# Splitting the first token block's hidden columns into two stretches around the second block, in a retention-plus-two-feed-forward kernel

## The chip, the cores and the metric

The kernel runs on one core of one Trainium2 chip. The metric is the device time of one execution in microseconds. Before the change the median of three runs is 911.7 us (911.51 to 911.89).

## What is computed

Three layers in float32, one after the other. Retention over 4 sequences of 768 tokens with 8 heads of width 64: per head `state = gamma*state + k v^T`, `y = scale * q state`. Then `x = elu(x @ w_in) @ w_out` with 512 to 2048 to 512 on all 3072 tokens. Then 512 to 1024 to 512 with `h * softmax(h)`, a layer norm over the 1024, a gain `g_ln`, and `@ w_out2`.

## The kernel before

**Arithmetic.** TensorE multiplies in fp32r. To keep float32 accuracy every operand is cut into a high part (a rounded copy) and a low part (the difference), and each product is three matmuls (`mm3`, lines 69 to 71). Weights arrive as raw 64-bit words, two uint32 each, and are made into float32 by bit operations. One weight tile (128x512) takes: a load on SP's queue (`load_w`, L97), absolute value on ScalarE (L102), a clamp on GpSimd (L103), three bit operations on VectorE (`bits_w`, L108 to L110), a high copy on ScalarE (`high_w`, L119) and a low difference on VectorE (`low_w`, L127). For the first feed-forward layer there are 32 such tiles: 16 of `w1i`, 16 of `w1o`.

**Retention.** The tokens of a sequence are cut into chunks of 64; a chunk of all heads is a *unit*, 48 in all, eight to a block of 512 tokens. For unit u: `scale_k` (GpSimd, L169), `att_scores` (TensorE, L175, L179), `att_mask` (VectorE, L183), `att_values` (TensorE, L216, L219), `att_done` (VectorE, L224, writes the unit's 64 columns of x), and `att_state` (VectorE L196, two small ScalarE copies L199, GpSimd L203). The state of unit u+1 needs that of unit u.

**First feed-forward layer.** Six blocks of 512 tokens, each 16 *steps*, one for each 128 hidden columns. Step s: `ff1_in` is 12 matmuls of 128x512 into a PSUM bank `hp`; `elu_a` to `elu_c` make the activation and its halves `gh` and `gl`; `ff1_out` of step s-2 (LAG = 2) adds 12 matmuls into `acc` (four banks that collect over the 16 steps of a block). After a block's last step the four banks are copied out by ScalarE and VectorE (L304, L306) and go to DRAM (`y_dr`).

**Order.** Everything stands in a `manual_schedule`: each engine issues its instructions in the order in which the program emits them, so an instruction that waits holds up all behind it on its engine; SP's DMA queue too. Tiles take any free buffer of their pool.

- Start: the eight units of block 0 in a loop (L442), with parts of three weights' conversion between them (`PRE`, `prep_w`) and the split of x in three pieces (`split_x0`, L244, L245), two of them on GpSimd. Units' inputs have four buffers and are loaded three units ahead.
- Block 0 (16 steps): two `prep_w` slots in every step convert two weights in a staggered manner: within a slot, the high copy of weight n-2, then the bit operations of n, then the low part of n-2. Every second step holds one unit of block 1. The activation goes by ScalarE twice (L262, L263), VectorE once (L272); `gl` by VectorE (L284).
- Blocks 1 to 5: the weights stay in SBUF. Every second step has one unit of the next block; `gl` by GpSimd. At the last step of a block the whole x of the next block is split: four ScalarE copies (L232), four VectorE differences (L237).
- Block 5 also converts the 16 weights of the second layer, one `prep_w` slot a step (those of `w_out2` are multiplied by the gain, L116), and reads back the first y tiles.
- Then the second feed-forward layer, 24 tiles of 128 tokens (`ff2_in`, `norm_a`, `norm_b`, `turn`, `turned`, `ff2_out`).

Of the kernel before, what the change touches and what calls it, by code (L numbers as in the profile page):

```python
# [18 lines left out]
P = 128  # L19
# [5 lines left out]
C = 64  # L25
# [10 lines left out]
HL = NF1 - 2  # L36
PRE = (2, 3, 4, 5)
AHEAD = 1
# [4 lines left out]
def tile_retention_ffn(ctx, tc, qkv, w_in1, w_out1, w_in2, w_out2, g_ln, dmask, odec, kdec, gdec, ident_in, out):  # L43
# [13 lines left out]
    xf = const.tile([P, KD, TB], F32, name="xf")  # L57
# [5 lines left out]

    t_dr = [dram.tile([4, 4, 32, 2 * P], F32, name=f"t_dr{i}") for i in range(3)]
# [8 lines left out]
    with tc.manual_schedule():  # L73
# [7 lines left out]
        x_p = ph1.enter_context(tc.tile_pool(name="x", bufs=1))  # L81
        e_p = ph1.enter_context(tc.tile_pool(name="e", bufs=3))
        g_p = ph1.enter_context(tc.tile_pool(name="g", bufs=3))
# [3 lines left out]
        stage_p = ph0.enter_context(tc.tile_pool(name="stage", bufs=4, side="right"))  # L87
# [18 lines left out]
        def bits_w(x):  # L106
            t, b = raw_t.pop(x), abs_t[x]
            nc.vector.tensor_scalar(b, b, 3, 0x3FFFFFF8, ALU.logical_shift_left, ALU.bitwise_and)  # L108
            nc.vector.scalar_tensor_tensor(b, t[:, :, 1], 0xC0000000, b, ALU.bitwise_and, ALU.bitwise_or)  # L109
            nc.vector.scalar_tensor_tensor(b, t[:, :, 0], 29, b, ALU.logical_shift_right, ALU.bitwise_or)  # L110
# [19 lines left out]
        def prep_w(order, n):  # L130

            at = lambda i: order[i] if 0 <= i < len(order) else None
            if at(n - 2):
                high_w(at(n - 2))
            if at(n + 1):
                clamp_w(at(n + 1))
            if at(n):
                bits_w(at(n))
            if at(n - 2):
                low_w(at(n - 2))  # L140
            if at(n + 3):
                load_w(at(n + 3))
# [19 lines left out]
        def load_unit(u):  # L162
            t = at_p.tile([P, 18 * D], F32, tag="in", name="in", bufs=4)
            nc.sync.dma_start(out=t, in_=qkv[u])
            in_t[u] = t
# [55 lines left out]
        def att_done(u, v):  # L221
            ci = u % UPB
            four = lambda t: t.rearrange("p (a o) t -> p a o t", a=2)
            nc.vector.tensor_tensor(four(xf[:, :, ci * C:(ci + 1) * C]), v[:, :, 2 * C:4 * C].rearrange("p a (o t) -> p a o t", o=2), four(od_sb), ALU.mult)  # L224

        x_t = {}

        def split_xh(tb, cs):
            if tb not in x_t:
                x_t[tb] = [x_p.tile([P, KD, TB], F32R, tag=tag, name=tag) for tag in ("xh", "xl")]  # L230
            for cc in cs:
                nc.scalar.copy(x_t[tb][0][:, cc], xf[:, cc])  # L232

        def split_xl(tb, cs):
            xh, xl = x_t[tb]
            for cc in cs:
                nc.vector.tensor_tensor(xl[:, cc], xf[:, cc], xh.bitcast(F32)[:, cc], ALU.subtract)  # L237


        def split_x0(ts, engine):  # L240
            if 0 not in x_t:
                x_t[0] = [x_p.tile([P, KD, TB], F32R, tag=tag, name=tag) for tag in ("xh", "xl")]
            xh, xl = x_t[0]
            nc.scalar.copy(xh[:, :, ts], xf[:, :, ts])  # L244
            engine.tensor_tensor(xl[:, :, ts], xf[:, :, ts], xh.bitcast(F32)[:, :, ts], ALU.subtract)  # L245
# [3 lines left out]
        def ff1_in(s):  # L249
            tb, f = divmod(s, NF1)  # L250
# [17 lines left out]
        def elu_b(s, on_act):  # L268
# [9 lines left out]
            if not on_act:  # L278
                elu_c(s, nc.gpsimd)
# [7 lines left out]
        def new_acc(tb):  # L287
            acc_t[tb] = [ps.tile([P, 2, 512], F32, tag="acc", name="acc", bufs=2) for _ in range(KD // 2)]

        def ff1_out(s):  # L290
            tb, f = divmod(s, NF1)
            if tb not in acc_t:
                new_acc(tb)
            wh, wl = w1o[f]
            gh, gl = g_t.pop(s)
            for m in range(KD):
                o = m * P
                mm3(acc_t[tb][m // 2][:, m % 2], wh[:, o:o + P], wl[:, o:o + P], gh, gl, f == 0, f == NF1 - 1)
            if f == NF1 - 1:
                for m in range(KD):  # L300
                    yt = yt_p.tile([P, TB], F32, tag="yt", name="yt", bufs=3) if m < 3 else e_p.tile([P, TB], F32, tag="e", name="yt")
                    src = acc_t[tb][m // 2][:, m % 2]
                    if m % 2:
# [3 lines left out]
                    nc.sync.dma_start(out=y_dr[tb][:, :, m, :].rearrange("c p t -> p c t"), in_=yt.rearrange("p (c t) -> p c t", c=CPB))  # L307
                del acc_t[tb]
# [30 lines left out]
        def norm_a(i):  # L339
            hp = h2.pop(i)  # L340
            st = sm_p.tile([P, 8], F32, tag="st", name="st")
            if i == 0:
                e, z = xf[:, :2], xf[:, 2:]
# [25 lines left out]
        def turn(i):  # L369
# [3 lines left out]
            t = z_p.tile([P, NF2 * P], F32, tag="t", name="t") if i else xf[:, :2].rearrange("p a b -> p (a b)")  # L373
# [51 lines left out]
        nc.gpsimd.memset(half_n, -0.5)  # L425
        load_unit(0)
# [7 lines left out]
        both = sets[0]  # L434
        scale_k(0)
# [4 lines left out]
        load_unit(2)  # L440
        slot = -1
        for u in range(UPB):  # L442
            nxt = sets[(u + 1) % 3] if u + 1 < UPB else both
            scale_k(u + 2)
            if u + 1 < UPB:
                att_scores(u + 1, nxt[0])
                att_mask(u + 1, nxt[1])
            if u + 3 < UPB + 3:
                load_unit(u + 3)
            if u < 2:  # L450
                load_w(order1[u])
# [4 lines left out]
            att_done(u, sets[u % 3][1])  # L456
            att_state(u + 1, nxt[1])
            if u in (3, 5, 7):
                split_x0(slice(0 if u == 3 else C * (u - 1), C * (u + 1)), nc.vector if u == 7 else nc.gpsimd)
            if u in PRE:  # L460
                prep_w(order1, slot)
                slot += 1


        NS = NB * NF1
        for s in range(NS + LAG):
            tb, k = divmod(s, NF1)
            u = UPB + AHEAD + s // 2 if s % 2 else (UPB if s == 0 else NU)
            if s < NS:
                ff1_in(s)  # L470
                elu_a(s, tb == 0)
                if k == NF1 - 1 and tb + 1 < NB:
                    split_xh(tb + 1, range(KD))
                    elu_b(s, tb == 0)
                    split_xl(tb + 1, range(KD))
            if u < NU:
                if u + 1 < NU:
                    att_scores(u + 1, both[0])
                att_values(u, both[0])
                if u + 1 < NU:  # L480
                    att_mask(u + 1, both[1])
                att_done(u, both[1])
                if u + 1 < NU:
                    att_state(u + 1, both[1])
                if u + 3 < NU:
                    load_unit(u + 3)
                if u + 2 < NU:
                    scale_k(u + 2)
            if tb == 0:
                prep_w(order1, slot)  # L490
                slot += 1
            if s < NS and (k < NF1 - 1 or tb + 1 == NB):
                elu_b(s, tb == 0)
            if s == NS + LAG - 2:
                ff2_in(0)
                norm_a(0)
                turn(0)
                turned(0)
                norm_b(0)
# [3 lines left out]
            if tb == 0:  # L503
# [131 lines left out]
```

## Time and profile before

| | |
|---|---|
| median of three runs | 911.7 us |
| the profiled execution's own time | 912.42 us |
| its span in the trace | 910.6 us |
| TensorE busy | 95% of the span, granted clock 0.979 in the mean |
| VectorE, ScalarE, GpSimd busy | 52%, 35%, 35% |

The 1.8 us between the span and the execution's time lie around the traced instructions. Shares of busy time are means over stages: block 0's steps lie between 37 and 159 us of the span, blocks 1 to 5 between 159 and 640, the second layer behind.

### The profile page before, as it was taken

What the parts mean: (1) busy time and instruction counts of PE and PEld (TensorE: products, weight loads), DVE (VectorE), ACT (ScalarE), POOL (GpSimd) and SP (SyncE); (2) the same over time, 40 slices, a digit from 0 to 9 for tenths busy, and PEclk for the clock granted to TensorE, in tenths of its full rate; (3) what the DMA queues carried; (4) which work ended last, traced back from release to release, by engine and by line L of the source; (5) the groups of instructions that cost most, each with busy time, mean ns of one, the idle gap of its engine ahead of it and who ended that gap; (6) DMA issues with size and microseconds to landing.
All of it is one profiled execution on the core that took longest, in us unless ns stands there. A gap on an engine that the chain in (4) does not pass through costs nothing.

```text
span 910.6 us, 15639 instructions
## 1 busy us (share of the span) xinstructions
PE 869.3 (95%) x6432; PEld 705.0 (77%) x6432; DVE 471.9 (52%) x781; ACT 320.2 (35%) x574; POOL 319.4 (35%) x319
## 2 busy tenths in 40 slices
PE   5588988999999999999999999999999999999998
PEld 4466766888888888888888887888778888888886
DVE  3589999422242223222432227899655555555442
ACT  3255555322232223222322223443333333333332
POOL 4434342333233323232333223455243333444330
PEclk9589999999999999999999999999999999999999
DMA  8445643211122111311131014330354444444432
GB/s 327 166 158 178 199 158 123 74 52 54 53 71 82 53 46 35 99 53 54 53 99 53 11 61 130 113 93 24 115 166 149 150 148 140 139 139 142 156 118 70
DMA packets 59879, 97.94 MB, mean 108 GB/s; under 512 B 4896, under 2 KB 41504, under 8 KB 59808
## 3 DMA queue, kind: packets, MB, share of 16 engines
q1 hardware_dynamic: 59808, 96.95, 32.5%
q8 instruction: 50, 0.82, 0.4%
q14 instruction: 21, 0.17, 0.1%
HBM read 72.29 MB, written 24.64 MB: 106 GB/s over the span
## 4 chain that ended last, share of the span: by engine, by line
PE 78%; DVE 14%; DMA 3%; issue 2%; ACT 1%; POOL 0%; SPq 0%; ACTq 0%; DVEq 0%; POOLq 0%
PE hp L70 12%; PE hp L71 12%; PE hp L69 12%; PE acc L69 9%; PE acc L70 8%; PE acc L71 8%; PE op L71 4%; PE op L69 4%; PE op L70 4%; DVE wt L109 3%; DVE wt L110 2%; PE ab L175 1%; DVE wt L108 1%; DMA in<-in_qkv 1%; DVE w1il L127 1%
## 5 line engine op out<-in xcount | busy, mean ns | idle before, releaser
L284 POOL TENSOR_TENSOR gl<-e,gh 128x512 fp32r<-128x512 f32 x80 | 107.5, 1344 | 225.0 <-issue 151.3
L71 PE MATMUL acc<-gh,w1ol 128*128 128x512 f32 x384 | 152.0, 396 | 8.1 <-DVE w1ol L127 8.1
L69 PE MATMUL hp<-xh,w1ih 128*128 128x512 f32 x384 | 152.2, 396 | 5.8 <-ACT xh L244 2.5
L69 PE MATMUL acc<-gh,w1oh 128*128 128x512 f32 x384 | 155.0, 404 | 2.0 <-ACT w1oh L119 2.0
L71 PE MATMUL hp<-xh,w1il 128*128 128x512 f32 x384 | 152.2, 396 | 1.0 <-DVE w1il L127 1.0
L70 PE MATMUL hp<-xl,w1ih 128*128 128x512 f32 x384 | 151.8, 395 | 0.9 <-DVE xl L237 0.9
L70 PE MATMUL acc<-gl,w1oh 128*128 128x512 f32 x384 | 151.0, 393 | 0.0
L265 ACT ACTIVATE e<-hp 128x512 f32<-128x512 f32 x80 | 47.8, 598 | 199.5 <-PE hp L71 197.7
L274 DVE TENSOR_SCALAR e<-e 128x512 f32<-128x512 f32 x80 | 35.5, 443 | 137.0 <-ACT e L265 137.0
L276 ACT CAST gh<-e 128x512 fp32r<-128x512 f32 x96 | 59.6, 621 | 118.9 <-DVE e L275 81.7
L71 PEld LDWEIGHTS acc<-gh,w1ol 128*128 128x128 f32 x384 | 72.8, 190 | 26.5 <-DVE w1ol L127 11.1
L183 DVE TENSOR_TENSOR pt<-ab,dm_sb 128x256 f32<-128x256 f32 x43 | 18.1, 422 | 142.5 <-PE ab L219 133.5
L69 PEld LDWEIGHTS hp<-xh,w1ih 128*128 128x128 f32 x384 | 73.4, 191 | 21.7 <-ACT xh L244 2.7
L71 PEld LDWEIGHTS hp<-xh,w1il 128*128 128x128 f32 x384 | 73.2, 191 | 19.2 <-DVE w1il L127 4.0
L69 PEld LDWEIGHTS acc<-gh,w1oh 128*128 128x128 f32 x384 | 72.5, 189 | 19.5 <-ACT w1oh L119 3.2
L70 PEld LDWEIGHTS hp<-xl,w1ih 128*128 128x128 f32 x384 | 73.3, 191 | 17.4 <-DVE xl L237 1.6
L70 PEld LDWEIGHTS acc<-gl,w1oh 128*128 128x128 f32 x384 | 72.7, 189 | 14.1
L354 POOL TENSOR_SCALAR z<-z,st 128x1024 f32<-128x1024 f32 x22 | 27.7, 1259 | 140.0 <-DVE st L352 140.0
L71 PE MATMUL op<-w2oh,zl 128*128 128x512 f32 (+1 forms) x192 | 74.2, 386 | 2.6 <-DVE zl L395 2.6
L69 PE MATMUL op<-w2oh,zh 128*128 128x512 f32 (+1 forms) x192 | 74.3, 387 | 0.6 <-ACT zh L389 0.6
L69 PE MATMUL hp<-w2ih,yh 128*128 128x512 f32 x192 | 74.7, 389 | 0.0
L70 PE MATMUL hp<-w2il,yh 128*128 128x512 f32 x192 | 74.7, 389 | 0.0
(112 smaller groups left out, 1408.2 us busy)
## 6 DMA issues: line engine op xcount, KB each, us to landing
in<-in_qkv SPq DMA_DIRECT2D x48, 576.0 KB, 4.2
raw<-in_w_in SPq DMA_DIRECT2D x24, 512.0 KB, 3.7
raw<-in_w_out SPq DMA_DIRECT2D x24, 512.0 KB, 3.5
t_dr<-t SPq DMA_DIRECT2D x22, 512.0 KB, 2.8
zt<-t_dr SPq DMA_DIRECT2D x88, 128.0 KB, 2.5
y_dr<-yt SPq DMA_DIRECT2D x24, 256.0 KB, 2.6
yin<-y_dr SPq DMA_DIRECT2D x24, 256.0 KB, 3.5
out<-ot SPq DMA_DIRECT2D x23, 256.0 KB, 2.7
```

What stands on the lines that cost most here:

```text
L69: nc.tensor.matmul(o, lh, rh, start=first, stop=False)
L70: nc.tensor.matmul(o, lh, rl, start=False, stop=False)
L71: nc.tensor.matmul(o, ll, rh, start=False, stop=last)
L108: nc.vector.tensor_scalar(b, b, 3, 0x3FFFFFF8, ALU.logical_shift_left, ALU.bitwise_and)
L109: nc.vector.scalar_tensor_tensor(b, t[:, :, 1], 0xC0000000, b, ALU.bitwise_and, ALU.bitwise_or)
L110: nc.vector.scalar_tensor_tensor(b, t[:, :, 0], 29, b, ALU.logical_shift_right, ALU.bitwise_or)
L183: nc.vector.tensor_tensor(pt, v[:, :, :2 * C], dm_sb, ALU.mult)
L265: nc.scalar.activation(e, h_t[s], AF.Exp)
L274: nc.vector.tensor_scalar(e, e, 1.0, -1.0, ALU.min, ALU.add)
L276: nc.scalar.copy(gh, e)
L284: engine.tensor_tensor(gl, e, gh.bitcast(F32), ALU.subtract)
L354: nc.gpsimd.tensor_scalar(z, z, st[:, 5:6], 1.0, ALU.add, ALU.mult)
```

## The change

The 96 steps of the first layer are ordered in segments: block 0's hidden columns 0 to 4, then the whole of block 1 (16 steps), then block 0's columns 5 to 15, then blocks 2 to 5. The sums of the first segment go to DRAM (`p_dr`, four tiles), are read back, and are added by VectorE when the third segment's banks are copied out. x is split unit by unit straight from `att_done`, and its two halves have two buffers each; the tile `xf` is gone. A generator deals a weight's work out in four parts (clamp of the next and first bit operation; second; third, the load of the weight three on, and the high copy; the low part), a number of parts at two places of a step: four and four in the first five steps, then four and two in even steps and two and two in odd ones through step 20. Before the first step one weight is converted instead of parts of three. All of block 0's units are loaded up front, in four buffers of a pool of their own and three others. Units of block 1 are worked in the first five steps (one in steps 0 and 1, two in steps 2 to 4), those of block 2 one a step in steps 21 to 28, the rest every second step.

```diff
-HL = NF1 - 2
-PRE = (2, 3, 4, 5)
-AHEAD = 1
+LEAD = 5
+SEGS = [(0, 0, LEAD), (1, 0, NF1), (0, LEAD, NF1)] + [(tb, 0, NF1) for tb in range(2, NB)]
+STEPS = [(i, tb, f) for i, (tb, a, b) in enumerate(SEGS) for f in range(a, b)]
...
-        x_p = ph1.enter_context(tc.tile_pool(name="x", bufs=1))
+        x_p = ph1.enter_context(tc.tile_pool(name="x", bufs=2))
...
-        stage_p = ph0.enter_context(tc.tile_pool(name="stage", bufs=4, side="right"))
+        stage_p = ph0.enter_context(tc.tile_pool(name="stage", bufs=3, side="right"))
...
+        def convert(order, held):
+            for n, x in enumerate(order):
+                if n:
+                    low_w(order[n - 1])
+                    yield
+                if n + 1 < len(order) and n + 1 != held:
+                    clamp_w(order[n + 1])
+                for i in range(3):
+                    bits_w(x, i)
+                    if i < 2:
+                        yield
+                if n + 3 < len(order):
+                    load_w(order[n + 3])
+                high_w(x)
+                yield
+            low_w(order[-1])
+
+        def run(turns, k):
+            for _ in range(k):
+                next(turns, None)
...
-        def att_done(u, v):
+        def att_done(u, v, engine):
...
+            xu = at_p.tile([P, KD, C], F32, tag="xu", name="xu")
+            nc.vector.tensor_tensor(four(xu), v[:, :, 2 * C:4 * C].rearrange("p a (o t) -> p a o t", o=2), four(od_sb), ALU.mult)
+            nc.scalar.copy(xh[:, :, ts], xu)
+            return lambda: engine.tensor_tensor(xl[:, :, ts], xu, xh.bitcast(F32)[:, :, ts], ALU.subtract)
...
+                    if i == 2:
+                        nc.vector.tensor_tensor(yt, src, back[m], ALU.add)
...
+                    if i == 0:
+                        nc.sync.dma_start(out=p_dr[m], in_=yt)
...
+        load_w(order1[0])
+        for u in range(2, UPB):
+            load_unit(u)
+        load_w(order1[1])
+        load_w(order1[2])
...
+            if u in (3, 4, 5, 6):
+                run(turns, 1)
...
+        slots = [(s, x) for s in range(LEAD) for x in (range(2) if s >= 2 * LEAD - UPB else range(1))]
+        slots += [(LEAD + NF1 + i, 0) for i in range(UPB)]
+        slots += [(s, 0) for s in range(2 * NF1, (NB - 1) * NF1, 2)]
...
+            if s <= END1:
+                run(turns, 4 if s < LEAD or s % 2 == 0 else 2)
...
+            if (s, 0) in bursts:
+                burst(bursts[s, 0])
...
+            if s <= END1:
+                run(turns, 4 if s < LEAD else 2)
+            if seg == 0:
                 elu_c(s, nc.vector)
+            if (s, 1) in bursts:
+                burst(bursts[s, 1])
```

## Rows read from the trace of the kernel before

**Rows 1.** The page: busy time of each engine, and the chain that ended last

```profile
PE 869.3 (95%) x6432; PEld 705.0 (77%) x6432; DVE 471.9 (52%) x781; ACT 320.2 (35%) x574; POOL 319.4 (35%) x319
PE 78%; DVE 14%; DMA 3%; issue 2%; ACT 1%; POOL 0%; SPq 0%; ACTq 0%; DVEq 0%; POOLq 0%
```

**Rows 2.** Windows: stretch, length, busy us (instructions) by engine, TensorE's granted clock, DMA

```profile
0.00:10.00 10.00, 3.62 (x94) 2.88 (x96) 1.73 (x5) 1.88 (x3) 2.56 (x9) 1.00 0.80 271
10.00:20.00 10.00, 7.59 (x253) 6.32 (x248) 5.43 (x13) 4.09 (x11) 5.71 (x9) 0.83 1.01 390
20.00:37.20 17.20, 6.31 (x193) 5.39 (x193) 11.75 (x21) 5.93 (x14) 12.94 (x13) 0.59 0.69 244
37.20:54.70 17.50, 13.94 (x152) 9.72 (x152) 9.12 (x14) 5.67 (x11) 4.86 (x5) 0.62 0.31 118
54.70:158.60 103.90, 93.12 (x765) 70.21 (x757) 100.62 (x159) 59.47 (x112) 35.66 (x37) 0.97 0.49 163
158.60:256.50 97.90, 97.46 (x864) 79.26 (x865) 32.15 (x67) 28.51 (x56) 29.38 (x30) 1.00 0.19 60
```

**Rows 3.** Waits of TensorE from 0 to 158.6 us: total, times, longest

```profile
PE acc L71 <- DVE w1ol L127: 8.1, 7, 1.5
PE ab L175 <- DMA in<-in_qkv: 5.1, 2, 4.7
```

**Rows 4.** Timeline of VectorE: states of the second and third unit

```profile
9.80 0.41 DVE L196 TENSOR_TENSOR state<-sg,acc 128x256 f32<-128x256 f32 x1
12.28 0.41 DVE L196 TENSOR_TENSOR state<-sg,acc 128x256 f32<-128x256 f32 x1
```

**Rows 5.** The chain that ended last, two steps of block 0

```profile
97.96 0.41 DVE pt L183
99.03 0.35 DVE wt L108
...
103.15 0.35 DVE wt L108
...
105.54 0.54 DVE gl L284
...
113.17 0.41 DVE pt L183
```

**Rows 6.** Groups of VectorE, 54 to 158 us: count, busy us, mean ns

```profile
L284 DVE TENSOR_TENSOR gl<-e,gh 128x512 fp32r<-128x512 f32 x14 | 15.0, 1070 | 0.0
L272 DVE SCALAR_TENSOR_TENSOR e<-e,hp 128x512 f32<-128x512 f32 x14 | 9.5, 675 | 0.0
```

**Rows 7.** Timeline of VectorE: a low part right behind its high copy

```profile
648.56 1.53 DVE L127 TENSOR_TENSOR w2ol<-wt,w2oh 128x512 fp32r<-128x512 f32 x1 [0.69 <-ACT w2oh L119]
```

**Rows 8.** Groups of VectorE, then of GpSimd, 596 to 638 us (block 5)

```profile
L110 DVE SCALAR_TENSOR_TENSOR wt<-raw,wt 128x512 uint32<-128x512 uint32 x8 | 12.6, 1580 | 0.3
...
L127 DVE TENSOR_TENSOR w2ol<-wt,w2oh 128x512 fp32r<-128x512 f32 x6 | 5.7, 956 | 0.0
L284 POOL TENSOR_TENSOR gl<-e,gh 128x512 fp32r<-128x512 f32 x8 | 13.3, 1664 | 18.3 <-issue 18.0 <-POOL yl L327 0.4
L103 POOL TENSOR_SCALAR wt<-wt 128x512 f32<-128x512 f32 x7 | 7.4, 1053 | 0.0
```

**Rows 9.** Timeline of TensorE: first matmuls of steps 30, 31 and 32

```profile
244.58 0.39 PE L69 MATMUL hp<-xh,w1ih 128*128 128x512 f32 x1
...
250.02 0.39 PE L69 MATMUL hp<-xh,w1ih 128*128 128x512 f32 x1
...
256.55 0.39 PE L69 MATMUL hp<-xh,w1ih 128*128 128x512 f32 x1
```

**Rows 10.** Timeline of TensorE: the first matmul of step 0

```profile
37.19 0.80 PE L69 MATMUL hp<-xh,w1ih 128*128 128x512 f32 x1 [2.55 <-ACT xh L244]
```

**Rows 11.** Timeline of TensorE: its waits at block 5's start and in the second layer

```profile
549.74 0.50 PE L70 MATMUL hp<-xl,w1ih 128*128 128x512 f32 x1 [0.45 <-DVE xl L237]
...
658.68 0.50 PE L71 MATMUL op<-w2oh,zl 128*128 128x512 f32 x1 [1.51 <-DVE zl L395]
```

More of the change, by code (lines that the diff above doesn't have):

```diff
@@ L285, in elu_c, with new_acc @@
             g_t[s] = (gh, gl)
-        def new_acc(tb):
-            acc_t[tb] = [ps.tile([P, 2, 512], F32, tag="acc", name="acc", bufs=2) for _ in range(KD // 2)]
+        def new_acc(i):
+            acc_t[i] = [ps.tile([P, 2, 512], F32, tag="acc", name="acc", bufs=2) for _ in range(KD // 2)]
         def ff1_out(s):
-            tb, f = divmod(s, NF1)
-            if tb not in acc_t:
-                new_acc(tb)
+            i, tb, f = STEPS[s]
+            _, f0, f1 = SEGS[i]
+            if i not in acc_t:
+                new_acc(i)
             wh, wl = w1o[f]
@@ L425, in tile_retention_ffn @@
         nc.gpsimd.memset(half_n, -0.5)
+        part = [wb_p.tile([P, TB], F32, tag="wb", name="part") for _ in range(KD)]
         load_unit(0)
@@ L434, in tile_retention_ffn @@
         both = sets[0]
+        turns = convert(order1, 1)
         scale_k(0)
@@ new lines, in tile_retention_ffn @@
+        first.close()
+        e_p = ph1.enter_context(tc.tile_pool(name="e", bufs=3, reuse_waits="tile"))
+        g_p = ph1.enter_context(tc.tile_pool(name="g", bufs=3, reuse_waits="tile"))
+        NS = len(STEPS)
+        slots = [(s, x) for s in range(LEAD) for x in (range(2) if s >= 2 * LEAD - UPB else range(1))]
+        slots += [(LEAD + NF1 + i, 0) for i in range(UPB)]
+        slots += [(s, 0) for s in range(2 * NF1, (NB - 1) * NF1, 2)]
+        bursts = dict(zip(slots, range(UPB, NU)))
@@ L466, in tile_retention_ffn, with burst @@
+        def burst(u):
+            if u + 1 < NU:
+                att_scores(u + 1, both[0])
+            att_values(u, both[0])
+            if u + 1 < NU:
+                att_mask(u + 1, both[1])
+            split = att_done(u, both[1], nc.vector)
+            if u + 1 < NU:
+                att_state(u + 1, both[1])
+            split()
+            if u + 3 < NU:
+                load_unit(u + 3)
+            if u + 2 < NU:
+                scale_k(u + 2)
+        END1 = LEAD + NF1 - 1
         for s in range(NS + LAG):
-            tb, k = divmod(s, NF1)
@@ L468, in tile_retention_ffn @@
-            u = UPB + AHEAD + s // 2 if s % 2 else (UPB if s == 0 else NU)
+            seg, tb, k = STEPS[s] if s < NS else (None, NB, s - NS)
+            on_act = seg in (0, 1)
             if s < NS:
                 ff1_in(s)
[L471 to L493, printed above, removed]
+            if s <= END1:
+                run(turns, 4 if s < LEAD or s % 2 == 0 else 2)
+            if s < NS:
+                elu_a(s, on_act)
+            if (s, 0) in bursts:
+                burst(bursts[s, 0])
+            if s < NS:
+                elu_b(s, on_act)
+                if seg != 0:
+                    elu_c(s, nc.gpsimd)
@@ L513, in tile_retention_ffn @@
                 yt_p = ph0.enter_context(tc.tile_pool(name="yt0", bufs=3, side="right", reuse_waits="tile"))
-            if u == NU - 1:
+                back = []
+                for m in range(KD):
+                    back.append(yt_p.tile([P, TB], F32, tag=f"back{m}", name="back", bufs=1))
+                    nc.sync.dma_start(out=back[m], in_=p_dr[m])
+            if bursts.get((s, 0)) == NU - 1:
                 ph0.close()
```

129 lines of the change are left out of this document (55 added, 74 removed).

## The prediction

> **What bounds the kernel now.** I read the page first [rows 1]: TensorE is busy 95% of the span and makes 78% of the chain that ended last, VectorE 14%. The mean hides stages, so the windows come next [rows 2]. From 158.6 us on TensorE has almost no gap (97.46 of 97.90 us at granted clock 1.00) and nothing but fewer matmuls would help. Ahead of that it is not the limit. Up to 37.2 us it works on units only, 17.5 us busy, at a clock of 0.59 in the end; from 37.2 to 54.7 its clock is 0.62; from 54.7 to 158.6 VectorE is busy 100.6 of 103.9 us. The waits say the same [rows 3]: TensorE waits for low parts of `w1o`, and at the start for units' inputs. A step of 24 matmuls costs 5.44 us at full clock (244.58 to 250.02) and a unit 1.09 more (250.02 to 256.55 less 5.44) [rows 9]. Block 0 with its eight units needs 16 x 5.44 + 8 x 1.09 = 95.8 us and takes 158.6 - 37.2 = 121.4. So 25.6 us are lost there, and up to 37.2 us in the start.
>
> The change can win only in these two places. It spreads most of the conversion over 16 more steps, which need no new weights at first.
>
> **VectorE's prices.** Two steps of block 0 go from one unit's mask (97.96) to the next's (113.17) [rows 5]: 15.21 us with four weights, one unit (97.96 to 99.03: 1.07) and two activations (0.68 + 1.07 each [rows 6]). A weight is (15.21 - 1.07 - 3.50) / 4 = 2.66 us. Undisturbed it is 2.39 (103.15 to 105.54) [rows 5]; the rest is GpSimd at work beside it. In block 5 the third bit operation takes 1.58 and the low part 0.96 [rows 8] where an operation of this size mostly takes 0.68 (as L272 does) [rows 6], so 2.39 + 0.90 + 0.28 = 3.57 is the worst that the trace shows.
>
> New: the low part now stands right behind the high copy on VectorE, with nothing between. The trace shows that place once: VectorE waits 0.69 us for ScalarE [rows 7]. So a dealt weight costs 2.66 + 0.69 = 3.35, with 3.08 and 4.26 as ends (below 3.08 only if other work came between, and the code puts none there).
>
> **The start.** The loads no longer wait for buffers, bar unit 7's, which waits on SP for unit 0's buffer, free before 10 us; behind it stand two weights that nothing wants before step 0. Eight units of 0.59 MB, one weight of 0.52 and 0.39 MB of constants are 5.6 MB; at 2.71 MB in the first 10 us and 3.90 in the next ten [rows 2] unit 7 is there at 17.5 us, two more weights and units 8 and 9 (2.2 MB) at 23.2. GpSimd stands at the scaling of unit 9 before block 0 is finished, so step 0 begins at 24 at the earliest. The states' chain is slower: unit 2's was done at 12.7 us, and its input now lies behind a weight (0.52 MB, 1.3 us). From 14.0 to the state of unit 8 are six more at 2.48 us or somewhat less [rows 4]; the two seen are 2.48 apart with a DMA wait between them, and I take 2.1: 26.6, and 0.4 for the last low part of x. Step 0 at 27 us. At the late end only the two weights that are no longer converted here come off: 37.2 - 2 x 2.66 = 31.9.
>
> **The first five steps.** VectorE: 10 weights x 3.35 = 33.5; 5 activations x 1.75 = 8.8; 8 units x (1.07 + 0.5), the 0.5 for the low part of x (256 columns: between the mask's 0.41 and the activation's 0.68 [rows 5, 6], less the overlap of neighbours) and a short wait for its high copy: 12.6. Sum 54.9. In step 0 VectorE also waits some 1.4 us for the first product, which runs at the low clock. 56.3 us; ends 53.6 (2.39) and 65.4 (3.57). TensorE has to do 5 first products, 3 second ones and 8 units in this time: 8 x 2.72 + 8.7 = 30.5 at full clock, 61 at half. Near half it would rule too; I take VectorE. Two units in one step wait for each other only through VectorE, whose work is counted. A unit's load now starts when the unit three before it is done, and its scaling stands half a step later on GpSimd, ahead of a clamp; a late landing would make that clamp and then VectorE late, which the upper end has to cover. Step 5 begins at 83.3 us.
>
> **Steps 5 to 20.** A step has 1.25 weights and one VectorE operation of the activation, while `gl` goes to GpSimd: 1.25 x 3.35 + 0.68 = 4.87, less than TensorE's 5.44. With weights as in block 5, where GpSimd also has `gl` (1.66) and a clamp (1.05) a step [rows 8], it is 1.25 x 4.26 + 0.68 = 6.0, 9 us too long over 16 steps. The dealing leaves little room at the end: the last `w1i` and the `w1o` of steps 18 and 19 come within a step of their use. I take 2 us of stall, between 0 and 9, and 2.5 us (0 to 5) for the clock, which is likely low when step 5 begins.
>
> How far GpSimd's work delays VectorE's is the open price. With GpSimd busy 35.66 us of 103.9 beside a full VectorE [rows 2], the 15.21 us of two steps hold 4 x 2.39 + 1.07 + 3.50 = 14.1 of undisturbed work and 5.2 us of GpSimd; only 1.1 us of the 5.2 were added, in block 5 about half of GpSimd's time. The Trainium skill, "SBUF — State Buffer", section "SBUF: two separate sides", says that VectorE and GpSimd take their shared port pair as an exclusive lock for a whole instruction, the other fully blocked. Added in full the two steps would be 19.3 us, and the trace agrees with that rule in part only.
>
> **Behind.** Up to the start of step 32 TensorE then does 27 first and 27 second products and 8 units: 27 x 5.44 + 8 x 1.09 = 155.6. So step 32 starts at 83.3 + 155.6 + 2.5 + 2 = 243.4. Before it started at 256.55, with one unit more ahead of it: 255.5. Gain 12.1 us.
>
> **The rest, near nothing.** Four copies of the first segment's sums (ScalarE) lie beside 2.72 us of the next first product; uncovered, some 1.2 us. Four stores and four loads of 256 KB are issued on SP where it has nothing urgent; the loads wait for the last weight's buffers and hold up unit 19's load, needed two steps later. Adding instead of copying out the third segment costs VectorE some 1.4 us where it is a third busy. The split per unit removes five bursts of eight operations at block ends; the one visible wait behind it at full clock is 0.45 us [rows 11], the earlier one lies inside the 121.4. In block 5 the 0.69 a weight makes VectorE late by up to 4 us; `gl` is needed some 6 us after it is made, so no stall. At the second layer's start two weights' work is gone from VectorE but it comes late: TensorE's 1.51 us wait there [rows 11] may go or grow; 0, between -1.5 and +2.
>
> **Sum.** 912.42 (the profiled execution) - 12.1 - 0.45 = 899.9. The median of the runs lies 0.7 lower, so 899.
>
> **Rivals.**
> A. Better: the wait for the high copy is hidden (10 x 0.69 = 6.9) and the start is bound by loads alone (3): 889. For it: ScalarE is a third busy. Against it: the order of the four parts.
> B. VectorE in the first five steps as disturbed as in block 5: 65.4 instead of 56.3: 908. For it: two units a step bring GpSimd more scaling. Against it: `gl` is not GpSimd's there, and in block 0 the disturbance was 0.27 a weight.
> C. The start does not come forward, so the change does not do there what it says: step 0 at 37 costs 10: 909. For it: the chain state to state stays. Against it: between 20 and 37.2 us VectorE was busy 11.75 us and GpSimd 12.94 [rows 2], with work most of which goes.
> D. Slower: GpSimd's operations block VectorE in full in steps 5 to 20. A step is 1.25 x 3.08 + 0.68 + 1.66 + 1.25 x 1.05 = 7.5, so 16 x 2.06 = 33 of stall instead of 2: 930. It decides from 6.4 us a step on, where the stall eats the 12.5 and the 2. For it: the third bit operation's 1.58 in block 5. Against it: only a fifth of GpSimd's time showed in block 0 and half in block 5. The Trainium skill's page named above, taken whole, says the same.
>
> **How the numbers follow.** Forecast 0.60, with 892 to 906 as its own range from the ends above; A 0.10; B 0.12; C 0.08; D 0.06; the rest lies between them. 888 to 911 leaves out D and the outer edge of A. A measurement of this kernel can tell about 0.2% from no change, so faster is below 909.9: the forecast, A, most of B and of C, 0.85. Same: 0.06, from the edges of B and C. Slower: 0.09, D and what of B and C falls together.
>
> **What would show it.** Step 0's first matmul at 27 (24 to 32) instead of 37.2 [rows 10]; the first matmul of block 1 at 83; step 32's first at 243; VectorE full from step 0 to 5 and not from 5 to 20; behind every high copy a VectorE wait of about 0.7. Wrong if the first five steps take over 68 us, if TensorE waits for weights by more than 9 us in all in steps 5 to 20, or if the second layer is longer by over 2 us.

## The result: 0.6% slower

Median 916.73 us (915.8 to 919.01) against 911.8 for the kernel before (four runs each; 911.7 is the median of the first three of before): ratio 1.0058, 95% interval 1.004 to 1.0077. The forecast was 899, so not even the sign was right. The profiled execution took 915.8 us, its span 914.0 us against 910.6.

**Profile after.** The page first, to be read against [rows 1]: VectorE's busy time and the chain by engine.

```profile
PE 868.7 (95%) x6432; PEld 706.6 (77%) x6432; DVE 498.0 (54%) x794; ACT 333.9 (37%) x606; POOL 327.1 (36%) x328
...
PE 67%; DVE 19%; ACT 6%; issue 4%; DMA 2%; SPq 1%; POOL 0%; ACTq 0%; DVEq 0%
```

TensorE's share of the chain fell from 78% to 67%; ScalarE, 1% before, has 6%. That is the trail: ScalarE was nowhere in the prediction's list of bounds.

Timeline of TensorE after: the first matmuls of steps 0, 5 (block 1's first), 6, 18, 20, 21, 32 and of the second layer, to be read with [rows 9, 10].

```profile
30.76 0.80 PE L70 MATMUL hp<-xh,w1ih 128*128 128x512 f32 x1 [1.31 <-ACT xh L248]
...
90.10 0.79 PE L70 MATMUL hp<-xh,w1ih 128*128 128x512 f32 x1 [4.07 <-ACT xh L248]
...
98.29 0.39 PE L70 MATMUL hp<-xh,w1ih 128*128 128x512 f32 x1
...
163.99 0.39 PE L70 MATMUL hp<-xh,w1ih 128*128 128x512 f32 x1
...
179.22 0.50 PE L70 MATMUL hp<-xh,w1ih 128*128 128x512 f32 x1 [1.99 <-ACT w1ih L124]
...
187.63 0.39 PE L70 MATMUL hp<-xh,w1ih 128*128 128x512 f32 x1
...
257.80 0.39 PE L70 MATMUL hp<-xh,w1ih 128*128 128x512 f32 x1
...
636.23 0.39 PE L70 MATMUL hp<-w2ih,yh 128*128 128x512 f32 x1
```

| | predicted | after | difference |
|---|---|---|---|
| step 0 begins | 27.0 | 30.76 | +3.8 |
| first five steps | 56.3 | 59.34 | +3.0 |
| steps 5 to 20 | 91.5 | 97.53 | +6.0 |
| steps 21 to 31 | 68.6 | 70.17 | +1.6 |
| step 32 begins | 243.4 | 257.80 | +14.4 |

Against the kernel before, step 32 is 2.3 us later (255.5 there without its extra unit) where 12.1 earlier was forecast. From there to the second layer 0.8 is won, in the second layer's first four products 2.0 is lost (43.55 us from the layer's first matmul to the first matmul of its fifth tile, 41.53 before; this stretch is what the texts below call the layer's start to its fourth product), and the rest is equal within 0.2: 2.3 - 0.8 + 2.0 - 0.2 = 3.3, the 3.4 by which the spans differ, within rounding.

The windows after (stretch, length, busy us by engine PE, PEld, DVE, ACT, POOL, granted clock, DMA), to be read with [rows 2]:

```profile
30.80:90.10 59.30, 40.41 (x576) 30.11 (x576) 47.36 (x82) 28.45 (x58) 19.74 (x24) 0.85 0.47 161
90.10:178.00 87.90, 85.79 (x360) 68.54 (x360) 67.44 (x86) 47.76 (x83) 36.82 (x34) 0.97 0.38 120
178.00:187.60 9.60, 7.97 (x24) 5.45 (x25) 7.66 (x11) 5.70 (x10) 4.30 (x4) 0.82 0.33 111
187.60:257.80 70.20, 70.20 (x762) 56.90 (x761) 33.67 (x61) 23.08 (x49) 24.57 (x25) 1.00 0.29 91
```

VectorE is not full in the first two lines: 47.36 of 59.30 and 67.44 of 87.90 us, while before it was 100.6 of 103.9. TensorE is, in the second: 85.79 of 87.90. From step 6 to step 17 it keeps its pace: 12 steps from 98.29 to 163.99, 5.44 us each but for one of 5.86. What steps 5 to 20 lose, 10.5 us over 16 x 5.44, lies at their two ends: 2.8 in step 5 (90.10 to 98.29, the granted clock at 0.50 up to 95), 0.7 in steps 7 and 18, and 7.0 in steps 19 and 20 (9.51 and 8.41 us), where the last weights come late. TensorE waits 1.99 us for one of them at 179.22, and behind that its granted clock is 0.82 in the mean (the third line).

All that time VectorE runs behind: it begins the activation of step 6 at 104.37, 6.1 us behind the step's first matmul, and that of step 18 at 175.09, 11.1 behind. So VectorE and the engines that it works with take more than 5.44 us a step, though VectorE has nearly a quarter of its time idle. It waits for ScalarE, and ScalarE for VectorE. VectorE's waits after, and then ScalarE's, both from 90 to 187 us:

```profile
DVE e L276 <- ACT e L267: 8.0, 9, 4.2
DVE w1ol L132 <- ACT w1oh L124: 7.1, 10, 0.9
DVE w1il L132 <- ACT w1ih L124: 6.2, 9, 0.7
```

```profile
ACT gh L280 <- DVE e L276: 15.1, 15, 1.8
ACT w1ih L124 <- DVE wt L114: 12.3, 6, 3.0
ACT w1oh L124 <- DVE wt L114: 10.7, 5, 3.0
```

One turn of this loop, in the timeline of VectorE and ScalarE after:

```profile
125.57 0.69 DVE L114 SCALAR_TENSOR_TENSOR wt<-raw,wt 128x512 uint32<-128x512 uint32 x1
126.30 0.62 ACT L124 CAST w1oh<-wt 128x512 fp32r<-128x512 f32 x1 [3.05 <-DVE wt L114]
...
126.83 0.59 ACT L266 ACTIVATE e<-hp 128x512 f32<-128x512 f32 x1
126.95 0.69 DVE L132 TENSOR_TENSOR w1ol<-wt,w1oh 128x512 fp32r<-128x512 f32 x1 [0.69 <-ACT w1oh L124]
127.45 0.63 ACT L267 ACTIVATE e<-e 128x512 f32<-128x512 f32 x1
128.12 0.69 DVE L276 SCALAR_TENSOR_TENSOR e<-e,hp 128x512 f32<-128x512 f32 x1 [0.47 <-ACT e L267]
```

ScalarE idles 3.05 us for the third bit operation; behind its high copy stand the two passes of the activation. VectorE idles 0.69 for the high copy and 0.47 for the second pass. Each holds up the other, by the order of two queues.

### The profile page after: what moved, and what is told of

It is laid out like the page before. It is cut to its first block, busy times and chain, and to the rows that moved or that the text cites. A ratio compares the mean times of both kernels' runs of the same rounds, so it can differ in the third digit from the quotient of the medians.

```text
span 914.0 us, 15679 instructions
## 1 busy us (share of the span) xinstructions
PE 868.7 (95%) x6432; PEld 706.6 (77%) x6432; DVE 498.0 (54%) x794; ACT 333.9 (37%) x606; POOL 327.1 (36%) x328
## 4 chain that ended last, share of the span: by engine, by line
PE 67%; DVE 19%; ACT 6%; issue 4%; DMA 2%; SPq 1%; POOL 0%; ACTq 0%; DVEq 0%
PE hp L71 10%; PE hp L72 10%; PE hp L70 10%; PE acc L70 7%; PE acc L72 6%; PE acc L71 6%; DVE wt L114 5%; PE op L72 4%; PE op L71 4%; PE op L70 4%; DVE wt L112 3%; DVE wt L110 3%; PE ab L191 1%; DVE e L276 1%; PE ab L235 1%
## 5 line engine op out<-in xcount | busy, mean ns | idle before, releaser
L286 POOL TENSOR_TENSOR gl<-e,gh 128x512 fp32r<-128x512 f32 x91 | 121.2, 1332 | 255.6 <-issue 156.9
L280 ACT CAST gh<-e 128x512 fp32r<-128x512 f32 x96 | 59.6, 621 | 130.1 <-DVE e L279 109.5
L269 ACT ACTIVATE e<-hp 128x512 f32<-128x512 f32 x75 | 44.7, 596 | 127.1 <-PE hp L72 100.4
L278 DVE TENSOR_SCALAR e<-e 128x512 f32<-128x512 f32 x75 | 42.1, 562 | 85.3 <-ACT e L269 85.1
L72 PE MATMUL hp<-w2ih,yl 128*128 128x512 f32 x192 | 74.8, 390 | 1.1 <-POOL yl L340 1.1
```

Of the source, the lines that this page charges most:

```text
L72: nc.tensor.matmul(o, ll, rh, start=False, stop=last)
L269: nc.scalar.activation(e, h_t[s], AF.Exp)
L278: nc.vector.tensor_scalar(e, e, 1.0, -1.0, ALU.min, ALU.add)
L280: nc.scalar.copy(gh, e)
L286: engine.tensor_tensor(gl, e, gh.bitcast(F32), ALU.subtract)
```

## Experiments

All ratios are to the kernel before, run on the same chip beside them (its medians there: 911.65 us for e1 to e4, 911.43 for e5 to e8, 910.52 for e9 to e12); the other columns are from one trace of each. e5 and e9 have the same code up to block 5, and their traces differ by 1.25 us in the start and by 0.8 in the first five steps: smaller differences between two traces say nothing. "Lost" is what step 0 to step 20 (16 steps where block 0 stands in order) take beyond TensorE's work at full clock: 8 x 2.72 + 8 x 1.09 + 16 x 5.44 = 117.5 us with two stretches; 30 x 2.72 + 8 x 1.09 = 90.3 in order (up to step 16 only 14 second products are done; the prediction's 95.8 had 16). "Step 32" is when step 32 begins (before: without the extra unit that it has done by then). "Tail" is from block 5's first matmul to the first matmul of the second layer's fifth tile; between step 32 and block 5 all of them take 291.4 us.

| | median us | ratio, interval | step 0 | first 5 steps | steps 5 to 20 | lost | step 32 | tail |
|---|---|---|---|---|---|---|---|---|
| before | 911.8 | 1 | 37.19 | in order: | 121.4 | 31.1 | 255.5 | 129.3 |
| after | 916.73 | 1.0058, 1.004 to 1.0077 | 30.76 | 59.3 | 97.5 | 39.4 | 257.8 | 130.6 |
| e1 | 918.92 | 1.0076, 1.0048 to 1.0104 | 31.24 | 53.9 | 99.3 | 35.6 | 254.5 | 135.8 |
| e2 | 914.11 | 1.0032, 1.0019 to 1.0045 | 31.07 | 59.6 | 94.9 | 37.0 | 255.9 | 130.4 |
| e5 | 910.63 | 0.9991, 0.9981 to 1.0002 | 30.97 | 53.7 | 92.9 | 29.2 | 247.8 | 136.6 |
| e9 | 902.7 | 0.9916, 0.9899 to 0.9932 | 29.72 | 53.0 | 92.8 | 28.3 | 245.7 | 126.9 |
| e4 | 927.55 | 1.0173, 1.0154 to 1.0192 | 31.11 | in order: | 138.7 | 48.4 | 269.1 | 129.8 |
| e7 | 910.58 | 0.9992, 0.9983 to 1.0001 | 30.98 | in order: | 118.1 | 27.8 | 246.4 | 136.0 |
| e10 | 901.09 | 0.9897, 0.9883 to 0.9912 | 30.73 | in order: | 118.4 | 28.1 | 246.5 | 127.6 |

**e1: the low part of a weight stands one weight later.**

```diff
-                if n:
-                    low_w(order[n - 1])
+                if n == 1 and held > 0:
+                    low_w(order[0])
                     yield
...
-                for i in range(3):
-                    bits_w(x, i)
-                    if i < 2:
-                        yield
+                bits_w(x, 0)
+                yield
+                bits_w(x, 1)
+                yield
+                if n > 1 or n and held < 0:
+                    low_w(order[n - 1])
+                    yield
+                bits_w(x, 2)
```

> Theory 1 (VectorE is lost to its wait of 0.69 us for every high copy, 30 times up to step 20): the low part of a weight moves behind the second bit operation of the next weight, so the waits go. Steps 0 to 4 shorten by about 10 x 0.69 = 7 us, a step from 5 to 20 falls from 5.96 us of VectorE to about 5.1, under TensorE's 5.44, so the 7 us of TensorE's waits between 169 and 185 us go too: 916.7 - 14 = 903. Rival (GpSimd's operations beside VectorE's set the pace, and fill the gaps): less than 4 us gained, 913 or more.

918.92 us: no gain, although the first five steps are 5.4 us shorter and VectorE waits for no high copy any more. Two things eat that gain. The larger lies far behind: the edit also changes how the second layer's weights are dealt in block 5, and the tail is 5.2 us longer; at step 32 the kernel is 3.3 us ahead of after. The other is what this experiment was for: in steps 5 to 20, which are 1.7 us longer, the waits came back under another name. VectorE's waits of e1, 85 to 184 us, then ScalarE's:

```profile
DVE e L280 <- ACT e L271: 24.4, 13, 4.8
```

```profile
ACT w1ih L124 <- DVE wt L114: 14.0, 6, 2.5
ACT gh L284 <- DVE e L280: 13.8, 16, 1.3
ACT w1oh L124 <- DVE wt L114: 12.1, 6, 2.5
```

ScalarE still holds the activation behind a high copy that waits for VectorE. In these steps the wait for the high copies was real but not the cause by itself.

**e2: the activation's ScalarE passes are emitted ahead of the weight's parts.**

```diff
-            if s <= END1:
-                run(turns, 4 if s < LEAD or s % 2 == 0 else 2)
             if s < NS:
                 elu_a(s, on_act)
+            if s <= END1:
+                run(turns, 4 if s < LEAD or s % 2 == 0 else 2)
```

> ScalarE's two activation passes of a step are issued ahead of the weight's absolute value and high copy. If VectorE's repeated 0.47 us waits for the second pass (ten in steps 5 to 20) are a cost of their own, 3 to 5 us less than the changed kernel: 912 to 914. If they only take the place of the wait for the high copy, which now comes later, no gain or a loss: 916 to 920.

914.11 us, still slower than before. VectorE's waits for exp shrank to one of 5.0 us, those for high copies grew from 13.3 to 16.6. One half of the loop was cut and the other took part of its place: steps 5 to 20 are 2.6 us shorter.

**e3: GpSimd's `gl` of block 1 given to VectorE.**

```diff
-                if seg != 0:
+                if seg not in (0, 1):
                     elu_c(s, nc.gpsimd)
...
-            if seg == 0:
+            if seg in (0, 1):
                 elu_c(s, nc.vector)
```

> In the second segment VectorE makes gl instead of GpSimd. Rival theory (GpSimd beside VectorE): the third bit operation falls from 1.66 us back to 0.69 in most of the 16 steps, 0.97 saved for 0.6 added, and a step gets 0.3 us shorter: 912 to 915. Theory 1: VectorE has 0.6 more a step at the same waits, and some of the 0.97 back: 915 to 922.

917.94 us (1.007, 1.0049 to 1.0091), as after within the intervals. This does not price GpSimd beside VectorE by itself: from 90 to 178 us the third bit operation falls from 1.06 to 0.82 us and the low part from 0.98 and 0.94 to 0.69, 9 us in all, but VectorE's own `gl` adds 9.6. What it shows is that the waits stay: 7.1 us for exp, 13.1 for high copies, where after has 7.5 and 12.0.

**e4: the two stretches undone,** start, split and dealing kept; the sums' way through DRAM goes with them, and block 0's 16 steps get eight parts each.

```diff
-SEGS = [(0, 0, LEAD), (1, 0, NF1), (0, LEAD, NF1)] + [(tb, 0, NF1) for tb in range(2, NB)]
+SEGS = [(tb, 0, NF1) for tb in range(NB)]
```

> The segments are undone (block 0 whole, then block 1; one unit every second step; eight parts of weights in each of the 16 steps), the start, the split of x per unit and the new dealing stay. Theory 1: a step of block 0 costs VectorE 2 x 3.4 + 1.4 + 1.0 = 9.2 us, 147 for 16, so block 1 starts at 178 and block 2 at 274 instead of 257.8: about 932. If the segments themselves are the loss (two units in a step, TensorE idle in the first five steps): not over 912.

927.55 us. With this dealing the two stretches are worth 1.1%, some 11 us: they hide part of a conversion that the dealing has made dear (48.4 us lost in order, 31.1 before).

**e5: e1 and e2 together.**

> Both edits of the first two experiments at once. Theory 2 (VectorE and ScalarE wait for each other in a loop: third bit operation, high copy, then the next step's two activation passes queued behind that copy, then VectorE's part of the activation; either edit alone only moves the wait): neither the wait for the high copy nor the one for the second pass is left, a step from 5 to 20 costs VectorE about 5.0 us, TensorE no longer waits there, and the first five steps take about 53: 901 to 906. Rival (GpSimd's operations beside VectorE's are the pace): not under 911.

910.63 us: the edits that alone gave +2.2 and -2.6 us against after give -6.1 together. At step 32, ahead of what e1's edit costs in the tail, they are 3.3 and 1.9 us ahead of after alone, and 10.0 together. In steps 5 to 20 they give +1.7 and -2.6 alone, -4.6 together. And ScalarE no longer waits for VectorE there but for TensorE, 16 times where after has it once (4.4 us). ScalarE's waits of e5, 84.7 to 177.6 us:

```profile
ACT e L270 <- PE hp L72: 32.7, 16, 4.8
```

So the loop is cut, and the first five steps are near the 53 expected (53.7). The time is not in the 901 to 906 expected. The second layer now starts at 629.82 (636.23 after, 634.66 before), but needs 45.96 us to its fourth product where before needed 41.53; block 5 too takes 90.62 us (539.20 to 629.82) where after needed 87.03. In block 5 only e1's edit acts, and e1 alone takes 90.63 there: with the low part put between the bit operations, ScalarE's high copy waits for VectorE and the next activation for that copy, now with the second layer's weights. Timeline of VectorE and ScalarE in block 5 of e5:

```profile
559.77 0.62 ACT L124 CAST w2ih<-wt 128x512 fp32r<-128x512 f32 x1 [2.28 <-DVE wt L114]
...
560.85 0.59 ACT L273 ACTIVATE e<-hp 128x512 f32<-128x512 f32 x1
561.47 0.46 DVE L282 TENSOR_SCALAR e<-e 128x512 f32<-128x512 f32 x1 [1.40 <-ACT e L273]
...
565.58 0.63 ACT L124 CAST w2ih<-wt 128x512 fp32r<-128x512 f32 x1 [2.28 <-DVE wt L114]
```

One step takes the two engines 565.58 - 559.77 = 5.81 us, more than TensorE's 5.44. So they fall behind step by step, and TensorE pays at the end of the block.

**e6: e5, and the low part of a unit's x moved behind the next work of VectorE.**

```diff
-            split()
...
+            return split
...
+            if late:
+                late()
+            late = burst(bursts[s, 0]) if (s, 0) in bursts else None
```

> As the one before, and the low part of a unit's x moves one VectorE operation or more behind its high copy, away from GpSimd's operation on the state. If the dearer units (2.1 us of VectorE instead of 1.57) cost what they seem to, 8 x 0.5 in the first five steps and 7 x 0.5 in the start: 5 to 8 us less than the kernel with both edits. If GpSimd's operation only collides with the next VectorE operation, nothing.

911.99 us (1.0006, 0.9995 to 1.0018): no gain where 5 to 8 us were expected. Where the split stands was not on the path.

**e7: e5 with block 0 in order** (e4's edit).

> Blocks in order as in the fourth experiment, with both edits to the dealing. Theory 2: the dealing's waits made up most of that kernel's loss, 16 steps x 2 weights x 0.69 less something for the activation: 17 to 22 us less than its 927.6, so 905 to 911; against the kernel with segments and both edits it shows what the segments are worth with cheap dealing. Rival: still over 920.

910.58 us, equal to e5. What two stretches were worth in e4 was the dealing's own waste; with the loop cut they are worth nothing that the runs can tell. e5 loses 23.2 us in the first five steps and 5.9 in the next sixteen, e7 27.8 in block 0.

**e8: e5 with e3's edit.**

> Both edits, and gl of the second segment by VectorE. If GpSimd beside VectorE is what is left of the loss: 2 to 5 us less than with both edits alone. If VectorE now has room in steps 5 to 20, the same within 2 us; if 0.6 a step more fills it, up to 5 us more.

911.43 us (1.001, 0.9995 to 1.0026): no gain; as in e3, VectorE gets GpSimd's work in exchange.

**e9: e5, and block 5 by the order of before:** one weight's slot a step, the high copy a step behind its bit operations.

```diff
+        def prep2(n):
...
+            if at(n - 1):
+                high_w(at(n - 1))
+            if at(n + 1):
+                clamp_w(at(n + 1))
+            if at(n):
+                for i in range(3):
+                    bits_w(at(n), i)
+            if at(n - 1):
+                low_w(at(n - 1))
...
-                norm_b(0)
                 turn(0)
                 turned(0)
-            if s == NS + LAG - 1:
+                norm_b(0)
                 split_y(2)
...
-                run(turns, 4)
+                prep2(k)
```

> Both earlier edits, and the second layer's weights converted in block 5 as before the change: one slot a step, the high copy a step behind its bit operations, the first y tile's turn ahead of its square, and the third y tile's split a step earlier. Theory (ScalarE's high copy, waiting for VectorE, stands ahead of the next step's exp, so VectorE comes late to the second layer): second layer's start to its fourth product 41.5 to 43 us instead of 45.96, no wait of VectorE over 0.6 us for exp in block 5, time 906.5 to 908.5. Rival (the second layer's start is late for another reason, the earlier steps having only moved the waits): 45 to 46 us again, time 910 to 911.

902.7 us: 7.8 below before on the same chip, 14 below after's median, and more than expected. Block 5 takes 87.04 us and the second layer's start 39.86 (624.12 to 663.98). Timeline of e9's block 5:

```profile
561.76 0.60 ACT L288 ACTIVATE e<-hp 128x512 f32<-128x512 f32 x1 [1.57 <-PE hp L72]
562.39 0.43 DVE L297 TENSOR_SCALAR e<-e 128x512 f32<-128x512 f32 x1
...
564.10 0.62 ACT L124 CAST w2ih<-wt 128x512 fp32r<-128x512 f32 x1
...
567.26 0.60 ACT L288 ACTIVATE e<-hp 128x512 f32<-128x512 f32 x1 [1.98 <-PE hp L72]
```

ScalarE's high copy no longer waits, and ScalarE waits for TensorE: 5.50 us a step, TensorE's pace. The block's end shows it in VectorE's first reduction of the second layer, here in e9: it waits for TensorE, 5.6 us behind the layer's start, while after it began at 645.37, 9.1 behind, and late.

```profile
629.76 1.22 DVE L380 TENSOR_REDUCE st<-hp 128x1 f32<-128x1024 f32 x1 [2.56 <-PE hp L72]
```

The 3.6 us of block 5 are the slot's, since `norm_b` and `split_y` stand behind it. How much of the 6.1 in the second layer's start their order gave, and how much the slot, was not separated.

**e10: e9 with block 0 in order.**

> The same, with block 0's sixteen steps in order. Theory (with the waits taken out of the conversion the two stretches are worth nothing): within 1 us of the kernel with two stretches, 906.5 to 908.5. Rival (the two stretches are worth something once the end is repaired too): 2 us or more above it, 909 to 911.

901.09 us; the intervals of e9 and e10 overlap, and if anything the blocks in order are faster. The two stretches give nothing here either. What is won against before (9.4 us by the medians, 12.0 by the two traces) is in the traces 9.0 up to step 32, 6.5 of it in the start, 1.7 in the tail and 1.2 behind. The windows of e9 (first five steps, steps 5 to 20), then of e10 (block 0):

```profile
29.70:82.70 53.00, 39.45 (x577) 29.52 (x577) 44.22 (x82) 28.41 (x59) 19.27 (x26) 0.88 0.53 173
82.70:175.50 92.80, 89.82 (x384) 72.89 (x385) 78.80 (x98) 52.97 (x93) 39.78 (x37) 0.98 0.40 130
```

```profile
30.70:149.10 118.40, 101.46 (x841) 77.69 (x841) 107.45 (x184) 70.19 (x131) 38.54 (x47) 0.94 0.53 166
```

In e10 VectorE is busy 107.45 of 118.40 us: it paces block 0. The stretches spread its work, but e9's first five steps still lose 22.5 us, with ten weights, five activations and eight units in them.

**e11: e9, and the high copy ahead of the next weight's first bit operation.**

```diff
+                if n > 1:
+                    high_w(order[n - 1])
...
-                high_w(x)
+                if n == 0:
+                    high_w(x)
```

> The two-stretch kernel with the repaired end, and a weight's high copy not behind its own third bit operation but ahead of the next weight's first. Theory (ScalarE still waits for VectorE ahead of the activation): VectorE's waits for exp in steps 5 to 20 fall from 9 us to under 4 and the stall at step 20 (5.67 us instead of 2.6) goes, 904 to 906.5. Rival (VectorE is full there and the waits only change their name): within 1 us of the kernel without this edit, 906.5 to 908.5.

901.94 us (0.9898, 0.9881 to 0.9915), overlapping with e9; VectorE's waits for exp are 9.3 us where e9 has 9.1. The theory fell: the edit did not take these waits away. ScalarE waits for TensorE ahead of the activation, 32.7 us in 16 waits here and 32.5 in e9, so in e9 it is not VectorE that holds ScalarE up.

**e12: e9 with GpSimd's clamp of the first layer's weights left out.**

```diff
-            nc.gpsimd.tensor_scalar(a.bitcast(F32), a.bitcast(F32), E_MAX, E_MIN, ALU.min, ALU.max)
+            if x[0] in ("w2i", "w2o"):
+                nc.gpsimd.tensor_scalar(a.bitcast(F32), a.bitcast(F32), E_MAX, E_MIN, ALU.min, ALU.max)
```

> The two-stretch kernel with the repaired end, GpSimd's clamp of the first layer's 32 weights left out (a step of the computation). Theory (GpSimd's passes beside VectorE stretch its bit operations, 1.08 to 1.12 us in the mean against 0.69 alone): the bit operations of steps 5 to 20 fall to 0.85 to 0.95, 32 weights save 0.4 to 0.6 us of VectorE each, and the time falls by 3 to 6 us to 902 to 905. Rival (the stretch is from gl alone, or hidden): bit operations as before within 0.05, time within 1 us of the kernel with the clamp.

903.97 us (0.9921, 0.9904 to 0.9938): no gain. Groups of VectorE, 82 to 175 us, of e9 and then of e12:

```profile
L114 DVE SCALAR_TENSOR_TENSOR wt<-raw,wt 128x512 uint32<-128x512 uint32 x20 | 22.4, 1119 | 0.0
...
L132 DVE TENSOR_TENSOR w1ol<-wt,w1oh 128x512 fp32r<-128x512 f32 x10 | 10.2, 1015 | 2.6 <-ACT w1oh L124 2.6
```

```profile
L115 DVE SCALAR_TENSOR_TENSOR wt<-raw,wt 128x512 uint32<-128x512 uint32 x20 | 22.4, 1120 | 0.0
L296 DVE SCALAR_TENSOR_TENSOR e<-e,hp 128x512 f32<-128x512 f32 x16 | 11.0, 686 | 13.7 <-ACT e L287 13.7
...
L133 DVE TENSOR_TENSOR w1ol<-wt,w1oh 128x512 fp32r<-128x512 f32 x10 | 6.8, 683 | 3.0 <-ACT w1oh L125 3.0
```

The clamp stretched the low parts (1.02 instead of 0.68), not the third bit operation, 1.12 us in both, which stands beside `gl`. The 6.3 us that VectorE saves on 20 low parts come back mostly as waits for exp (13.7 instead of 9.1): from step 7 to step 19 TensorE takes 5.44 us a step in both kernels and sets the pace.

## Why the prediction was wrong

**The step that failed is "Steps 5 to 20".** It is the largest single miss, 6.0 of the 14.4 us up to step 32. The clock at its start cost 2.8 us where 2.5 was taken; the stall at its end cost 7.0 where 2 was taken. The step priced VectorE at 4.87 us, below TensorE's 5.44, and the trace has 5.96: VectorE's activation of step 5 at 97.04, that of step 20 at 186.45, so 89.4 / 15. The groups of VectorE after, 90 to 178 us, against [rows 5, 6, 8]:

```profile
L114 DVE SCALAR_TENSOR_TENSOR wt<-raw,wt 128x512 uint32<-128x512 uint32 x18 | 19.2, 1064 | 0.4
L112 DVE SCALAR_TENSOR_TENSOR wt<-raw,wt 128x512 uint32<-128x512 uint32 x18 | 13.6, 757 | 0.6
L110 DVE TENSOR_SCALAR wt<-wt 128x512 uint32<-128x512 uint32 x18 | 10.9, 603 | 0.0
...
L132 DVE TENSOR_TENSOR w1ol<-wt,w1oh 128x512 fp32r<-128x512 f32 x9 | 8.8, 978 | 6.5 <-ACT w1oh L124 6.5
```

A weight is 1.06 + 0.76 + 0.60 + 0.98 + 0.69 of wait = 4.09 us, not 3.35, near the 4.26 that the prediction held as its upper end. Two things are in it. GpSimd's `gl` and clamp stretch the four operations, which the prediction knew from [rows 8] but took by block 0, where VectorE makes `gl`; the nearer row was block 5. And VectorE waits. The stretch alone passes: in e9, without the waits, a weight is 1.08 + 1.12 + 0.42 + 1.0 = 3.62, a step 1.25 x 3.62 + 0.69 = 5.2 us, under 5.44, and TensorE keeps 5.44 to 5.54 us a step up to step 19. The waits alone would be the forecast's own 4.87; no run has them without either the stretch or VectorE's own `gl`. With both it is 1.25 x 4.09 + 0.68 = 5.8, and the waits for exp on top (8.0 - 4.2 us behind the first, 0.25 a step) make it about 6.0, where 5.96 was measured.

**What it left out is ScalarE's order.** The prediction asked what is late behind VectorE's wait for the high copy, not what stands behind the high copy on ScalarE while that waits for VectorE. It used ScalarE only once, as "a third busy" in rival A's favour. e1, e2 and e5 show that this place decides: in steps 5 to 20 the two edits together save 4.6 us where their sum alone is 0.9. Step 20 of e9 still takes 8.8 us, 3.4 too many; TensorE waits 1.92 us in it for a high copy of `w1o`. That part is left with the loop cut, and no run removed it.

**The range.** Nearly every term came in on its late side, and the four large ones stayed inside their ends. The late ends of the start, the first five steps, steps 5 to 20 and the second layer add up to 4.9 + 9.1 + 9.5 + 2 = 25.5 us; the range to 911 left room for 12 above 899, as if the terms would not go wrong together. None of the three signs of being wrong came either: the first five steps took 59.3 us, TensorE's waits for weights in steps 5 to 20 were 3.3 us (7.0 with what steps 19 and 20 lost at the lower clock), the second layer is 1.8 us longer. So the sum failed too, not only the step.

**The start:** 30.76, inside its 24 to 31.9, but 3.8 later than taken. VectorE wrote unit 2's state at 13.52 and unit 8's at 30.19: six states 2.78 us apart in the mean, where 2.1 was taken and [rows 4] had 2.48. The gain of 6.4 us on 37.19 is real, and each later version has it. Rival C fell in its strong form.

**The first five steps:** 59.3 instead of 56.3. The wait's price was right: VectorE waited 6.8 us for the ten high copies where 6.9 was counted. Units were dearer: the low part of x takes 0.78 us in the mean and 0.95 with the idle time ahead of it, not 0.5 with its wait. Ahead of the first unit VectorE idles 2.93 us where 1.4 was taken. VectorE's activation was cheaper, 0.68 + 0.68 us instead of 1.75.

**Behind:** 70.17 us for eleven steps and eight units instead of 68.6; a unit there costs 1.3, not 1.09. The prediction took the unit's price from a row of before with one unit every second step; why it is dearer with one in every step was not taken apart.

**The rest:** block 5's own wait went, as forecast (0.8 for 0.45). The second layer's start lost 2.0 us, the upper end of the range given. That block 5 "makes VectorE late by up to 4 us" was right: VectorE's first reduction of the second layer begins 9.1 us behind the layer's start, 5.6 before. "So no stall" was right for block 5 itself (87.03 us), but the lateness arrives in the second layer. TensorE's waits there, after, to be read with [rows 11]:

```profile
654.53 0.50 PE L72 MATMUL hp<-w2ih,yl 128*128 128x512 f32 x1 [1.12 <-POOL yl L340]
...
660.45 0.50 PE L70 MATMUL op<-w2oh,zh 128*128 128x512 f32 x1 [0.60 <-ACT zh L403]
661.71 0.50 PE L72 MATMUL op<-w2oh,zl 128*128 128x512 f32 x1 [0.53 <-DVE zl L409]
```

**The rivals.** B's price, 65.4 us for the first five steps, did not come. D had the right place (steps 5 to 20 and VectorE) and the wrong mechanism: 5.96 us a step, not 7.5, and in e9 GpSimd's stretch is all there (a weight's four operations 3.62 us, 3.40 after) while TensorE keeps its pace. The chance of 0.09 for slower was too small: all rivals but D were about sizes, and none was a loop between two queues.

**What stays open:** most of the 22.5 us that the first five steps lose in e9. TensorE's work, 30.5 us at full clock, takes 39.45 there at a granted clock of 0.88, so 9.0 us are the clock's and 13.5 are idle. One piece of the idle time can be read from e9's trace: VectorE's longest wait from 29.7 to 82.7 us, and TensorE's longest.

```profile
DVE wt L110 <- POOL wt L104: 5.4, 1, 5.4
```

```profile
42.36 0.80 PE L72 MATMUL hp<-xh,w1il 128*128 128x512 f32 x1 [3.70 <-DVE w1il L132]
```

VectorE waits 5.4 us for GpSimd's clamp of a weight, the clamp waits for ScalarE's absolute value, and that stands on ScalarE behind the activation of step 0, which begins at 35.57 when TensorE's first product is done: e2's edit put it there. TensorE then lacks for 3.70 us the low part of the weight before, which e1's edit has put behind the first two bit operations of the clamped one. So the cure for steps 5 to 20 made a wait in steps 0 and 1. No run put only this absolute value back ahead of the activation.

## What to carry to other kernels

When a producer on one engine and its consumer on another are moved next to each other, list what stands behind both in their queues: two engines that hand work to and fro in program order can each have idle time and still pace the kernel, and taking out one half of such a loop can show little (here +1.7 and -2.6 us alone, -4.6 together). Read each edit by stages: e1 won 3.3 us in the first layer and looked like a loss, because the same edit cost 5.2 at the end. Distance between the hand-overs counted for more than an even spread: in order, block 0 lost 31.1 us with `prep_w`, which keeps it, 48.4 with the new dealing, which has none (e4), and 27.8 with both edits (e7). When most terms of a forecast can come out late together, as here, add up the late ends too. And before work is spread to hide a cost, ask whether the cost was there before the edit: the two stretches were worth 11 us against the new dealing and nothing against a good one.

## What the hardware showed unasked

Two operations on VectorE and GpSimd can cost their sum. Timeline of both in e9:

```profile
118.33 1.72 POOL L305 TENSOR_TENSOR gl<-e,gh 128x512 fp32r<-128x512 f32 x1
118.83 1.77 DVE L114 SCALAR_TENSOR_TENSOR wt<-raw,wt 128x512 uint32<-128x512 uint32 x1
```

Alone they take 1.29 (the mean of GpSimd's seven `gl` from 200 to 240 us before, where no weight is converted) and 0.69 us, in a row 1.98; side by side 118.33 to 120.60, 2.27, but there `gl` begins while VectorE's low part of 117.80 still runs, up to 118.90. In e12 the pair overlaps that low part less and takes 118.40 to 120.42, 2.02 us. By the Trainium skill, "SBUF — State Buffer", section "SBUF: two separate sides", the two engines take their shared ports as an exclusive lock when VectorE's operation has two SBUF inputs, as here, and GpSimd's reads SBUF: the second is blocked until the first is done. For this pair the trace agrees: side by side costs the sum. Yet e12 shows that such a price can lie wholly beside the path.
